# One more yield ahead of the packed values' products, in the attention that runs beside the mix products

## The chip, the cores and the metric

The kernel runs on one core of one Trainium2 chip. The metric is the device time of one execution in microseconds; the time of a kernel is the median of its runs. Five engines take part: TensorE (PE, with its weight loads as PEld), VectorE (DVE), ScalarE (ACT), GpSimd (POOL) and SyncE (SP), whose queue here only issues transfers.

## The reference

Three layers follow one another, for 8 batches of 576 tokens. The change lies in the first; what matters of it:

```python
def sm_attn(qq, kk, vv):
    s = scale * np.matmul(qq, kk.transpose(0, 1, 3, 2))
    s = s - np.max(s, axis=-1, keepdims=True)
    a = np.exp(s)
    a = a / (np.sum(a, axis=-1, keepdims=True) + 1e-09)
    return np.matmul(a, vv)
p_packed = sm_attn(p, k, v)        # 32 packed rows for each of 8 heads
out = sm_attn(q, p_packed, p_packed)
```

The second layer takes the real part of a Fourier transform over tokens and channels, adds it to its input, norms the sum, and sends it through two matrices with a rectifier between (512 to 2048 to 512). The third routes each token to one of eight experts and runs the expert's two matrices.

## The kernel before

Batch 0 is computed first, by its own function. From then on TensorE runs through a list of mixes: mix b is the second layer's pair of matrices for 512 tokens of batch b, and two half mixes (R0, R1) take the tokens that are left over of four batches each. A mix has 16 blocks `f`. `mm1` computes `hp` (L1193: 12 products of 128x128 by 128x512 out of `ut`, the normed and transposed tokens), ScalarE and VectorE rectify and split it into `ht` (L1200, L1201), and two blocks later `mm2` adds it into the four `acc` (L1213: 12 products). Values are held as two float16 parts, a high and a low one, so each product is done in three passes. After the last block VectorE adds the four `acc` to the tokens (L1221).

The attention and the Fourier part of batch b+1 are a Python generator, `attention(b + 1)`, that runs in the background of mix b. While the mix emits its products, `tick` is called after each third of a block; it advances the background generators to their next `yield`. The attention's rate is `ATT_RATE = 2.3` steps for 12 mix products. A `yield` so decides how many mix products stand between two steps of the attention in the order of the program. The framework then schedules each engine's instructions from this order, by priorities (`high_priority` lifts a few), and inserts the semaphores. When a mix begins, what is left of the last attention is emitted in one go (`drain`).

In the attention, heads are handled in two groups of four (`hf` 0 and 1). In order: the scores of the packed rows (`scores`, L385), their maximum and exponentials, a transpose of the exponentials by SP's queue (`et`, L408), and the packed values: `pps`, 30 products for each half (L440) of `et` and of `vhl`, the values split in two float16 parts by ScalarE (L428) and VectorE (L430). `split_q` splits the queries (ScalarE L363, GpSimd L364; only from batch 2 on), `load_q` loads them. Then come the second attention (`eh`, made by ScalarE and GpSimd at L561 and L563, and its products `bp` at L590), the Fourier part (`P` at L650 and L655, `X` at L660 and L705), its sum with the tokens (L711), and `norm`: statistics (L738, L739), `rstd` (L740, L742), the normed rows `un` (VectorE L746), their split (ScalarE L750, GpSimd L751) and the transpose into `ut` by SP's queue (L753). `ut` of batch b+1 is what mix b+1 reads.

During mix 0 the weights of the second layer are still being made: VectorE decodes them tile by tile (L311, L313, L315) and splits them (L281, `w`), together with ScalarE (L279). Later mixes read them ready, and other background work (the experts' weights, L337 to L342) runs instead. `after_mix` computes the routing logits (`lp`, L1241) and writes the tokens to `XS` (L1258, L1259, L1271).

Of the kernel before, what the change touches and what calls it, by code (L numbers as in the profile page):

```python
# [192 lines left out]
def _build(tc, nc, ctx, A, stop):  # L193
# [152 lines left out]
    def attention(b):  # L346
# [5 lines left out]
        def load_q(hf):  # L352
            qt = ap.tile([128, 2, 710], F32, tag="qkv", name=f"q{b}_{hf}", bufs=2)
            nc.sync.dma_start(qt, A["qd"][b, :, 2 * hf:2 * hf + 2])
            q32.append(qt)

        def split_q(hf):
            qt = q32[hf]
            if b < PLAIN:
                return  # L360
            pool, tag = (ap, "vhl") if hf else (wp, "UT")
            qh = pool.tile([128, 2, 2, 710], F16, tag=tag, name=f"qh{b}_{hf}", bufs=2 - hf)
            nc.scalar.copy(qh[:, 0], qt)  # L363
            nc.gpsimd.tensor_tensor(qh[:, 1], qt, qh[:, 0], op=ALU.subtract)  # L364
            qts.append(qh)
# [60 lines left out]
        for hf in range(2):  # L426
            vh = ap.tile([128, 2, 5, 256], F16, tag="vhl", name=f"vhl{b}_{hf}")
            nc.scalar.activation(vh[:, 0], vts[hf], AF.Copy, scale=256.0)  # L428
            yield
            nc.vector.scalar_tensor_tensor(vh[:, 1], vts[hf], 256.0, vh[:, 0], ALU.mult, ALU.subtract)  # L430
            load_q(hf)
            yield
            if hf == 1:
                split_q(0)
                yield
            n = 0
            for t in range(5):
                for (x, y) in PASS:
                    for h in range(2):
                        nc.tensor.matmul(pps[64 * h:64 * h + 64, 128 * hf:128 * hf + 128],  # L440
                                         ets[hf][:, 5 * x + t, 64 * h:64 * h + 64],
                                         vh[:, y, t, 128 * h:128 * h + 128], start=n == 0, stop=n == 14,
                                         skip_group_check=True)
                    n += 1
            yield
# [179 lines left out]
        for t in (2, 0, 1) if b % 4 == 3 else (0, 1, 2):  # L625
# [73 lines left out]
            for lu, ut in ((1, uu), (0, ul)):  # L699
                if t < 2:  # L700
                    for n in range(6):
                        hf, x, y = terms[n]
# [983 lines left out]
    for b in [0, 1, 2, "R0", 3, 4, 5, 6, "R1", 7]:  # L1686
# [16 lines left out]
        if not isinstance(b, str):  # L1703
            if b + 1 < NB:
                ga = attention(b + 1)
                bg.append([ga, 0.0, ATT_RATE])
            if b == 1:
                bg.append([ew, 0.0, EW_RATE])
            if b == 7:
                actx.close()  # L1710
                open_moe()
                drain(ew)
                drain(last)
                r0 = routing(0)
                bg.append([r0, 0.0, R0_RATE])
# [99 lines left out]
```

## Time and profile before

| | |
|---|---|
| median of 3 runs | 1394.88 us (1393.84 to 1395.7) |
| the profiled execution | 1394.49 us |
| its span | 1392.5 us |
| TensorE busy | 1358.9 us, 98% of the span |
| VectorE, ScalarE, GpSimd busy | 50%, 37%, 28% |
| mean granted TensorE clock | 0.995 |

The span is the time from the first to the last recorded instruction. A busy share is a mean over the whole program; which engine the others wait for differs from stage to stage, and the list of waits and the timeline of a stage tell it. In a timeline a row may stand for several instructions of a kind (x12), and the brackets at its end give the engine's idle time before it and what ended that.

### The profile page before, as it was taken

How to read it: one execution, taken by the hardware profiler on the slowest of the kernel's cores; microseconds unless marked ns; L12 is line 12 of the kernel's file. 1: busy time of each engine (PE TensorE's matmuls, PEld its weight loads, DVE VectorE, ACT ScalarE, POOL GpSimd, SP SyncE). 2: the span in 40 equal slices, each digit the busy share in tenths (PEclk: the TensorE clock that was granted, in tenths of full speed). 3: DMA queues.
4: the chain of work that ended last, by engine and by line, in shares of the span. 5: the costliest groups of instructions: out<-in, count | busy, mean ns of one | idle time of the engine just before them, and what ended most of it. 6: DMA issues, size and time to landing. Idle time of an engine off the chain costs nothing. (4 is left out here: it accounts for less than half of the span.)

```text
span 1392.5 us, 29837 instructions
## 1 busy us (share of the span) xinstructions
PE 1358.9 (98%) x11860; PEld 785.9 (56%) x11860; DVE 696.1 (50%) x1478; ACT 515.2 (37%) x949; POOL 389.4 (28%) x388
## 2 busy tenths in 40 slices
PE   7999999999999999999999999999999999999998
PEld 4554445445564544544544556445777777777675
DVE  6889857657534656665665654443841111111111
ACT  3533265455355545545545545211211111111111
POOL 2002244343422443444344343001122211212101
PEclk8999999999999999999999999999999999999999
DMA  7466395684567557658557456245959668958783
GB/s 267 173 221 188 92 253 141 159 233 124 134 177 212 160 140 218 158 148 223 145 151 206 131 144 167 62 184 150 289 126 331 153 192 247 262 144 234 240 268 128
DMA packets 219648, 256.75 MB, mean 184 GB/s; under 512 B 151663, under 2 KB 163055, under 8 KB 216816
## 3 DMA queue, kind: packets, MB, share of 16 engines
q1 hardware_dynamic: 213424, 235.39, 59.8%
q0 software_dynamic: 6080, 19.40, 4.3%
q8 instruction: 95, 1.56, 0.5%
q14 instruction: 49, 0.40, 0.1%
HBM read 267.52 MB, written 52.95 MB: 230 GB/s over the span
## 5 line engine op out<-in xcount | busy, mean ns | idle before, releaser
L1213 PE MATMUL acc<-w,ht 128*128 128x512 f16 x1728 | 414.2, 379 | 0.0
L1193 PE MATMUL hp<-ut,w 128*128 128x512 f16 (+1 forms) x1536 | 364.4, 378 | 4.3 <-DVE w L281 2.0
L1193 PEld LDWEIGHTS <-w 128*128 128x128 f16 x1920 | 181.2, 98 | 183.0 <-issue 9.3
L1213 PEld LDWEIGHTS <-ht 128*128 128x128 f16 x1728 | 164.0, 98 | 188.5 <-issue 10.2
L339 POOL TENSOR_TENSOR halfs<-stage,halfs 128x512 f16<-128x512 f32 x128 | 155.2, 1221 | 285.7 <-ACT halfs L338 269.0
L1631 PE MATMUL ehp<-xgt,w1b 128*128 128x128 f16 (+1 forms) x3936 | 218.5, 215 | 2.9 <-remote 1.7
L1631 PEld LDWEIGHTS <-w1b 128*128 128x128 f16 x3936 | 209.8, 98 | 18.1 <-issue 4.5
L1663 PE MATMUL eo<-w2b,hx 128*128 128x512 f16 (+1 forms) x984 | 209.5, 380 | 0.0
L1648 DVE SCALAR_TENSOR_TENSOR hx<-ehp,hx 128x512 f16<-128x512 f32 x76 | 52.4, 691 | 308.0 <-ACT hx L1647 283.7
L1201 DVE SCALAR_TENSOR_TENSOR ht<-hp,ht 128x512 f16<-128x512 f32 (+1 forms) x160 | 101.4, 634 | 163.3 <-ACT ht L1200 162.4
L1200 ACT ACTIVATE ht<-hp 128x512 f16<-128x512 f32 (+1 forms) x160 | 88.0, 550 | 243.8 <-PE hp L1193 238.7
L1663 PEld LDWEIGHTS <-hx 128*128 128x128 f16 (+1 forms) x984 | 87.2, 99 | 95.5 <-issue 4.4
L1673 POOL DMA_INDIRECT out<-ys,sidx x38 | 40.4, 1064 | 320.5 <-ACT ys L1672 300.3
L1647 ACT ACTIVATE hx<-ehp 128x512 f16<-128x512 f32 x76 | 45.3, 597 | 160.7 <-PE ehp L1631 154.1
L1672 ACT ACTIVATE ys<-eo,scl 128x512 f32<-128x512 f32 x38 | 26.1, 687 | 174.0 <-PE eo L1663 173.3
L338 ACT CAST halfs<-stage 128x512 f16<-128x512 f32 x128 | 77.1, 616 | 9.3 <-DMA WS<-halfs 5.9
L337 ACT ACTIVATE stage<-stage 128x512 f32<-128x512 f32 x128 | 77.5, 623 | 0.3
L1587 POOL DMA_INDIRECT xg<-XS,gidx x38 | 40.4, 1064 | 101.4 <-DVE sidx L1553 51.5
L364 POOL TENSOR_TENSOR qh<-q,qh 128x1420 f16<-128x1420 f32 x12 | 34.6, 2885 | 51.9 <-ACT qh L363 51.9
L1193 PE MATMUL hp<-utr,w 128*128 128x256 f16 x384 | 47.2, 273 | 0.5 <-DVE ht L1201 0.5
L555 POOL TENSOR_TENSOR eo<-ee 128x256 f32<-128x256 f32 (+1 forms) x21 | 21.0, 1001 | 59.9 <-DVE ee L539 59.3
L751 POOL TENSOR_TENSOR unh<-un,unh 128x512 f16<-128x512 f32 x28 | 31.9, 1159 | 18.3 <-ACT unh L750 14.6
(399 smaller groups left out, 1332.8 us busy)
## 6 DMA issues: line engine op xcount, KB each, us to landing
w1b<-WS SPq DMA_DIRECT2D x156, 512.0 KB
w2b<-WS SPq DMA_DIRECT2D x156, 512.0 KB
stage<-in_w SPq DMA_DIRECT2D x64, 512.0 KB
WS<-halfs SPq DMA_DIRECT2D x128, 256.0 KB
q<-in_qd SPq DMA_DIRECT2D x16, 710.0 KB
v<-in_vd SPq DMA_DIRECT2D x16, 640.0 KB
k<-in_kd SPq DMA_DIRECT2D x16, 576.0 KB
XS<-xh SPq DMA_DIRECT2D x36, 256.0 KB
```

The costliest lines, as they stand in the source:

```text
L337: nc.scalar.activation(st[:, a], st[:, a], AF.Copy, scale=64.0 if k < 4 else 256.0)
L338: nc.scalar.copy(so[:, 0], st[:, a])
L339: nc.gpsimd.tensor_tensor(so[:, 1], st[:, a], so[:, 0], op=ALU.subtract)
L1193: nc.tensor.matmul(hp[:, c0:ntok], w12[:, f, 0, x, 128 * c:128 * c + 128], ut[:, 4 * y + c, c0:ntok], start=n == 0, stop=n == 11, skip_gro ...
L1200: pace[1] = nc.scalar.activation(ht[:, 0, :ntok], hp[:, :ntok], AF.Relu).ins
L1201: pace[0] = nc.vector.scalar_tensor_tensor(ht[:, 1, :ntok], hp[:, :ntok], 0.0, ht[:, 0, :ntok], ALU.max, ALU.subtract).ins
L1213: nc.tensor.matmul(self.acc[j], ht[:, x, 128 * j:128 * j + 128], w12[:, f, 1, y], start=f == 0 and n == 0, stop=f == 15 and n == 2)
L1587: nc.gpsimd.indirect_dma_start(out=g_, out_offset=None, in_=XS[0:rows], in_offset=bass.IndirectOffsetOnAxis(ap=gidx[:, b:b + 1], axis=0), ...
L1631: latest[0] = nc.tensor.matmul(hp[:, cols], w1b[r][:, 2 * c + fg, x, 128 * f:128 * f + 128], xt[b][:, 4 * y + c, rows], start=c + n == 0 a ...
L1647: nc.scalar.activation(ht[:, fg, 0], hp, AF.Relu)
L1648: nc.vector.scalar_tensor_tensor(ht[:, fg, 1], hp, 0.0, ht[:, fg, 0], ALU.max, ALU.subtract)
L1663: latest[0] = nc.tensor.matmul(op[rows], h[:, f // 4, x, c0 + rows.start:c0 + rows.stop], w2b[r + a][:, f, y], start=n == 0, stop=n == 23, ...
```

## The change

It adds a `yield` in front of the packed values' products: for the second heads in every batch of the generator (1 to 7), and for the first heads in batches 4 to 7. Two lines are added, so that every later line has a number greater by two.

```diff
             if hf == 1:
                 split_q(0)
                 yield
+            if hf == 1 or b >= 4:
+                yield
             n = 0
             for t in range(5):
                 for (x, y) in PASS:
```

How the order of the instructions changes is seen at three places. The first is TensorE in batch 5, between the first heads' packed values (`vhl_0`) and the second heads' (`vhl_1`); `hp_4`, `hp_5` and `acc_5902` to `acc_5905` are the mix's tiles, `lp` the routing logits. Weight loads and repeats are left out. Before:

```order
L440 MATMUL pps_5993<-vhl_0_5994,et_0_5938 64x128
...
L1193 MATMUL hp_4_6043<-ut_5522,w_130 128x512
...
L1213 MATMUL acc_5902<-w_130,ht_2_5890 128x512
...
L1213 MATMUL acc_5904<-w_130,ht_2_5890 128x512
L440 LDWEIGHTS et_1_5971
L440 MATMUL pps_5993<-vhl_1_6054,et_1_5971 64x128
```

After:

```order
L442 MATMUL pps_5993<-vhl_0_5994,et_0_5938 64x128
...
L1195 MATMUL hp_4_6013<-ut_5533,w_130 128x512
...
L1215 MATMUL acc_5902<-w_130,ht_2_5890 128x512
...
L1215 MATMUL acc_5905<-w_130,ht_2_5890 128x512
...
L1245 MATMUL lp_6090<-wgh,xt_5964 128x9
...
L1195 MATMUL hp_5_6102<-ut_5533,w_130 128x512
L442 LDWEIGHTS et_1_5971
L442 MATMUL pps_5993<-vhl_1_6063,et_1_5971 64x128
```

Between the two halves stood 12 `hp` and 9 `acc` products; now 6 `hp`, 12 `acc` and 9 `hp` products do, with the routing logits among them.

The second place is VectorE at the end of batch 1's attention, which runs beside mix 0: the statistics, `rstd` and the two `un` of the batch's last two tiles, and the adds of mix 0's four accumulators (`acc_670` to `acc_673`). Before:

```order
L738 BN_STATS bst_1_0_1455<-ul_1_1348 128x6
L738 BN_STATS bst_1_1_1458<-uu_1_1349 128x6
L739 BN_AGGR mv_1_1453<-bst_1_0_1455 128x2
L739 BN_AGGR mv_1_1453<-bst_1_1_1458 128x2
L740 TENSOR_SCALAR rstd_1_1454<-mv_1_1453 128x2
L746 TENSOR_SCALAR un_1_0_1475<-ul_1_1348,mv_1_1453,rstd_1_1454 128x512
L746 TENSOR_SCALAR un_1_1_1487<-uu_1_1349,mv_1_1453,rstd_1_1454 128x512
...
L1221 TENSOR_TENSOR ul_0_457<-ul_0_457,acc_670 128x512
```

After:

```order
L740 BN_STATS bst_1_1_1467<-uu_1_1356 128x6
L741 BN_AGGR mv_1_1462<-bst_1_0_1464 128x2
L1223 TENSOR_TENSOR ul_0_457<-ul_0_457,acc_670 128x512
L741 BN_AGGR mv_1_1462<-bst_1_1_1467 128x2
L1223 TENSOR_TENSOR uu_0_458<-uu_0_458,acc_671 128x512
L742 TENSOR_SCALAR rstd_1_1463<-mv_1_1462 128x2
L1223 TENSOR_TENSOR ul_1_459<-ul_1_459,acc_672 128x512
L748 TENSOR_SCALAR un_1_0_1481<-ul_1_1355,mv_1_1462,rstd_1_1463 128x512
L748 TENSOR_SCALAR un_1_1_1494<-uu_1_1356,mv_1_1462,rstd_1_1463 128x512
L1223 TENSOR_TENSOR uu_1_460<-uu_1_460,acc_673 128x512
```

Three of the four adds now stand ahead of the two `un`; before, all four stood behind them.

The third place is TensorE over the same stretch, from the batch's last X product to the first product of mix 1 (`hp_0`); `ht_13` to `ht_15` are the last blocks of mix 0, `s_2_0_0` the scores of batch 2. Before:

```order
L705 MATMUL X_1_1_1411<-pph,big_957 128x128
L1213 LDWEIGHTS ht_13_1465
L1213 MATMUL acc_673<-w_130,ht_13_1465 128x512
...
L660 MATMUL X_2_1512<-pph,big_957 32x256
...
L385 MATMUL s_2_0_0_1658<-k_0_1654,p_1651 32x288 x4
L1213 LDWEIGHTS ht_15_1569
L1213 MATMUL acc_671<-w_130,ht_15_1569 128x512
...
L1193 MATMUL hp_0_1584<-ut_1322,w_130 128x512
```

After:

```order
L707 MATMUL X_1_1_1418<-pph,big_969 128x128
L1215 LDWEIGHTS ht_14_1505
L1215 MATMUL acc_673<-w_130,ht_14_1505 128x512
...
L662 MATMUL X_2_1515<-pph,big_969 32x256
...
L1215 MATMUL acc_671<-w_130,ht_15_1568 128x512
...
L385 MATMUL s_2_0_0_1658<-k_0_1654,p_1651 32x288 x4
L1195 LDWEIGHTS w_130
L1195 MATMUL hp_0_1584<-ut_1331,w_130 128x512
L385 MATMUL s_2_0_1_1659<-k_0_1654,p_1651 32x288 x4
```

The last X product has moved towards the end of the mix: 27 mix products stood between it and `hp_0` before, 13 do now, and one of the score groups stands behind the first product of `hp_0`.

## Rows read from the trace of the kernel before

**Rows 1.** The profile page: span, and busy time of each engine
```profile
span 1392.5 us, 29837 instructions
...
PE 1358.9 (98%) x11860; PEld 785.9 (56%) x11860; DVE 696.1 (50%) x1478; ACT 515.2 (37%) x949; POOL 389.4 (28%) x388
```

**Rows 2.** TensorE's waits: line, releaser, total us, times, longest us
```profile
PE hp L1193 <- DVE w L281: 2.0, 2, 1.8
...
PE pps L440 <- DVE vhl L430: 1.7, 2, 1.3
PE bp L590 <- POOL eh L563: 1.7, 2, 0.9
...
PE pps L440 <- DMA et<-ehl: 1.3, 1, 1.3
```

**Rows 3.** Timeline, batches 2 and 4: start, us, engine, work, [idle before, releaser]
```profile
195.77 0.97 PE L440 MATMUL pps<-vhl,et 128*64 128x128 f16 x28 [0.45 <-DVE vhl L430]
...
440.75 1.03 PE L440 MATMUL pps<-vhl,et 128*64 128x128 f16 x30 [1.33 <-DMA et<-ehl]
...
443.12 1.49 DVE L430 SCALAR_TENSOR_TENSOR vhl<-v,vhl 128x1280 f16<-128x1280 f32 x1 [3.01 <-ACT vhl L428]
443.13 1.37 ACT L363 CAST qh<-q 128x1420 f16<-128x1420 f32 x1
...
446.35 1.03 PE L440 MATMUL pps<-vhl,et 128*64 128x128 f16 x30
```

**Rows 4.** Timeline, batch 5, second heads
```profile
544.92 0.72 ACT L1258 ACTIVATE xh<-uu,rsc 128x512 f16<-128x512 f32 x1 [2.15 <-DMA XS<-xh]
...
548.55 1.49 DVE L430 SCALAR_TENSOR_TENSOR vhl<-v,vhl 128x1280 f16<-128x1280 f32 x1 [1.53 <-ACT vhl L428]
...
550.10 0.97 PE L440 MATMUL pps<-vhl,et 128*64 128x128 f16 x28 [1.28 <-DVE vhl L430]
```

**Rows 5.** Timeline, mix 0: twelve mix products in a row
```profile
109.43 2.75 PE L1213 MATMUL acc<-w,ht 128*128 128x512 f16 x12
```

**Rows 6.** Timeline, the turn from mix 0 to mix 1
```profile
161.57 8.38 SPq L753 DMA_TRANSPOSE ut<-unh  x4
...
164.13 3.41 PE L1213 MATMUL acc<-w,ht 128*128 128x512 f16 x15
164.81 0.55 DVE L746 TENSOR_SCALAR un<-ul,mv,rstd 128x512 f32<-128x512 f32 x1 [0.81 <-POOL rstd L742]
...
166.15 2.27 POOL L751 TENSOR_TENSOR unh<-un,unh 128x512 f16<-128x512 f32 x2 [1.22 <-ACT unh L750]
...
167.36 0.69 DVE L1221 TENSOR_TENSOR ul<-ul,acc 128x512 f32<-128x512 f32 x1
...
167.47 0.69 PE L385 MATMUL s<-k,p 64*32 64x288 f32 x8
...
168.09 1.90 PE L1213 MATMUL acc<-w,ht 128*128 128x512 f16 x8
...
171.91 1.89 PE L1193 MATMUL hp<-ut,w 128*128 128x512 f16 x8 [1.92 <-DMA ut<-unh]
```

**Rows 7.** Windows, mix 0: stretch, length, busy PE PEld DVE ACT POOL, clock, DMA share, GB/s
```profile
106.00:118.00 12.00, 12.00 (x58) 5.13 (x54) 12.00 (x18) 4.99 (x7) 1.55 (x1) 1.00 0.50 181
...
142.00:154.00 12.00, 11.79 (x78) 6.56 (x75) 11.57 (x20) 6.08 (x12) 1.79 (x1) 1.00 0.50 171
```

**Rows 8.** The same windows at the program's start and at the turn of mix 0
```profile
25.00:30.00 5.00, 3.49 (x7) 2.52 (x8) 4.76 (x11) 1.10 (x2) 1.23 (x2) 0.50 0.38 127
30.00:35.00 5.00, 5.00 (x23) 2.85 (x22) 4.79 (x10) 1.18 (x2) 0.85 (x4) 0.74 0.00 0
...
170.00:175.00 5.00, 3.09 (x19) 1.17 (x20) 3.64 (x9) 0.00 (x0) 0.00 (x0) 1.00 0.28 53
```

**Rows 9.** Timeline, a later turn (SP's queue and TensorE)
```profile
720.93 3.49 SPq L753 DMA_TRANSPOSE ut<-unh  x2
...
730.32 2.75 PE L1193 MATMUL hp<-ut,w 128*128 128x512 f16 x12
```

## The prediction

> **What bounds the kernel now.** The page comes first: TensorE is busy for 1358.9 us of a span of 1392.5 us, every other engine for half of it or less [rows 1]. The rest, 33.6 us, is all that any order of the same work can win, so the question is only which TensorE waits the change takes away and which it makes. The list of waits by engine and line names them [rows 2]. At the line of the packed values (`pps`) TensorE waits three times: twice for `vhl`, the split of the values, 1.7 us together, and once for `et`, the transposed exponentials, 1.3 us. Exactly: 0.45 us in batch 2, 1.33 us before the first heads of batch 4 [rows 3] and 1.28 us before the second heads of batch 5 [rows 4]; 3.06 us in all. All other entries of that list are waits of the mix, of the Fourier part or of the turn from one mix to the next.
>
> A step of the attention generator is handed out per 12/2.3, about 5 to 6, mix products, and 12 such products take 2.75 us with the last one's own time, some 0.22 us each [rows 5]. One extra yield is therefore some 1.3 us of TensorE work that has no need of the attention.
>
> **The change, part by part.** It adds or removes no instruction. TensorE's busy time stays at 1358.9 us; the sum is made of waits alone.
>
> Second heads, all batches. In batch 5, 21 mix products stand between the two halves of `pps` in the order of before and 27 after, six more, 1.3 us. The wait there is 1.28 us, because ScalarE stood 2.15 us for a buffer that a transfer to XS had to free, and so the split on VectorE ran only from 548.55 us to 550.04 us [rows 4]. ScalarE and VectorE do not wait for the first half of `pps` here, so the split ends at the same time and the six products lie in front of it: −1.28 us. Batch 2 likewise, −0.45 us. Batches 3, 6 and 7 have no wait there to lose.
>
> First heads, batches 4 to 7. In batch 4 the first heads' products wait 1.33 us for `et` [rows 3]; six products of 1.3 us go ahead of them: −1.33 us, and nothing in batches 5 to 7, where TensorE did not wait. There is a price in batch 4: ScalarE now has the split of q (`qh`, 1.37 us at 443.13 us) ahead of the split of the second heads' values, which costs VectorE's split the same 1.37 us of delay; it had landed at 444.61 us against products at 446.35 us, a margin of 1.74 us, and six products more. I take nothing for it, and 1.0 us as the other end.
>
> Later steps. All that follows in the attention moves back by 6 products (batches 2 and 3) or 12 (4 to 7): the loads of q, p, k and v on SP's queue, the splits on ScalarE and GpSimd, the second attention and the Fourier part. The transfers are for a batch that TensorE reads tens of us later. What stands at the end is the turn: the next mix's first product needs `ut`, the transposed norm. At the tightest turn of batches 2 to 7, SP's last transposes end at 724.42 us and the mix starts at 730.32 us [rows 9]; with the 1.96 us from the end of issue to landing that the turn of mix 0 shows (below) there are 3.9 us left, and the Fourier part moves by 9 products, 2 us. I take nothing; the three other turns of this kind have more room, and two are followed by a half mix, whose products need another `ut`.
>
> Batch 1, whose attention runs beside mix 0, is where I see a loss. It too gets the yield before the second heads, but it has no room. VectorE decodes the weights there and is busy for 12.00 of 12 us and still 11.57 of 12 later [rows 7], and TensorE's waits of mix 0 come of it: 2.0 us for weight tiles, 1.8 us of them at one place, and 1.7 us for `eh`, which ScalarE and GpSimd make of what VectorE hands on [rows 2]; 3.7 us in all. The change moves each of these places. In the order of after, VectorE does the split of that one weight tile before it waits for the next stage, so that I take its 1.8 us as gone; the others, 1.9 us, I leave, since their cover is the same in steps and VectorE is as full. Bounds: 1.0 us left (half of the others goes too) to 3.7 us (nothing goes).
>
> The turn of mix 0 then costs more. Before, TensorE waited 1.92 us for `ut` [rows 6]. The chain: VectorE writes the normed rows `un` at 164.81 us, ScalarE and GpSimd split them until 168.42 us, SP transposes them until 169.95 us, and the product starts at 171.91 us: 7.1 us from the start of `un`. TensorE had 15 + 8 products and 8 score products (0.69 us) [rows 6] besides the P and X products to fill it. After, 13 mix products instead of 27 stand behind the last X of the batch; and in VectorE's order the two `un` now stand behind three of mix 0's closing adds (0.69 us each, as the one at 167.36 us), the third of which needs the products of `ht_15` up to the third column block. So `un` can't start before TensorE has only 3 products (0.66 us) and four score products (0.35 us) left. From there: one add 0.69 + 0.2 to see it, 7.1 us of chain, against 1.0 us of cover: a wait of 7.0 us in place of 1.92 us, +5.1 us. With mix 0's other waits at 1.9 us in place of 3.7 us (−1.8 us) that is +3.3 us; with the bounds above +2.4 to +5.1 us, and +1.9 us if the add is not in the way.
>
> A small wait may appear at one of the many moved places; I take one of the size of the shorter `vhl` wait, +0.4 us, 0 to 1.0 us.
>
> Sum: −3.06 + 3.3 + 0.4 = +0.6 us on the profiled execution's 1394.49 us: 1395.1 us. The median of the runs is 0.39 us above that execution, so 1395.5 us. The low ends (+1.9 and 0) give −1.2 us, 1393.7 us; the high ones (+5.1, 1.0, and 1.0 for batch 4) +4.0 us, 1398.9 us.
>
> **A rule to weigh.** What would a wait of 7 us do to TensorE's clock? The granted clock was 1.00 (2.4 GHz) in the stretch with the wait of 1.92 us [rows 8]; near the start, where TensorE was busy for only 3.49 us of 5, it was 0.50 (1.2 GHz), and it came back within the following 5 us of full work (0.74 on the mean, so 2.6 us at half). A loss of that sort after the turn would cost half of 2.6, 1.3 us. The Trainium skill ("TensorE: Matmul & The Clock Gate", section "The HAM clock gate (the "warmup" mystery)") says that an idle TensorE falls to half clock and that activity has to release it again. By that rule the change is dearer by those 1.3 us; by the row of the 1.92 us wait it isn't. The forecast leaves the loss out, because the score products split the wait.
>
> **The rivals.** (A) *Faster.* The moved places in mix 0 lose nearly all their waits, as batch 1's steps no longer meet VectorE's late tiles, and the turn grows less, to 5.5 us, as the transposes meet an emptier queue: −3.7 + 3.6 − 3.06 = −3.2 us, 1391.7 us with the median's 0.39 us. For it: the largest wait of mix 0 goes by the order itself. Against: VectorE is full from 106 to 154 us [rows 7], and the chain from `un` has no slack that a queue could give. It decides once mix 0 with its turn costs less than +0.3 us net.
>
> (B) *Slower by the clock.* The turn's wait of 7 us drops the clock, 1.3 us, and mix 0 keeps its other waits: +5.1 + 1.3 + 0.4 − 3.06 = +3.7 us, 1398.6 us. At most, if half clock holds for the 5 + 2.6 us that it does in [rows 8], 3.8 us instead of 1.3 us: 1401.1 us. It decides once the wait at the turn is seen with a granted clock below 1.
>
> (C) *Slower by the tiles.* VectorE's full stretch of mix 0 gets the norm and the adds later, and new waits for weight tiles appear, two of the size of the 1.8 us: +3.3 + 3.5 + 0.4 − 3.06 = +4.1 us, 1399.0 us. For: VectorE is saturated from 106 to 154 us; against: in before one tile alone came late by more than 0.3 us.
>
> (D) *The change doesn't do what it says.* The splits move along with the products (ScalarE does `vhl` of the second heads only when it sees the first half of `pps` end, as in batch 4, where its copy of them starts behind the first half), and half of the 3.06 us remains: +1.5 us on the forecast, 1397.0 us.
>
> **How the numbers follow.** Forecast 0.52, A 0.14, B 0.13, C 0.10, D 0.11. What a measurement can tell from no change is about 0.2%, 2.8 us: faster is below 1392.1 us, slower above 1397.7 us. Of the forecast's 0.52, 0.05 ends above and 0.01 below; of A's 0.14, 0.11 is faster; of B and C together, 0.20 is slower; of D, 0.02. Faster 0.12, slower 0.27, the rest, 0.61, the same. The range leaves out A's far end and the dear end of B and C: 1391.9 to 1399.2 us. The forecast alone: 1393.7 to 1398.9 us.
>
> **What would show it.** Right: no wait of over 0.3 us at the `pps` line of batches 2, 4 and 5; a wait for `ut` of about 7 us at the end of mix 0, with VectorE's `un` behind the third closing add; the wait of 1.8 us for a weight tile gone; from the second mix on, the same sequence of waits as before less those three. Wrong: a turn below 5 us (then A); a granted clock below 1.00 in the 5 us behind the turn (B); more than 3.7 us of waits in mix 0 ahead of the turn (C); a split of `vhl` that starts later beside its products (D). The forecast fails above all if the turn's chain is shorter than the one I copy from before.

## The result: 0.56% slower, outside the range

The changed kernel takes 1400.68 us (median of 5 runs, 1399.69 to 1401.8) against 1393.9 us for the kernel before in runs taken with it (1391.84 to 1395.7): a ratio of 1.0056 with a 95% interval of 1.0043 to 1.0068. Forecast were 1395.5 us and a range up to 1399.2 us. The profiled execution took 1400.68 us.

The page of the changed kernel, its span and TensorE's busy time, against [rows 1]:

```profile
span 1398.9 us, 29822 instructions
...
PE 1361.6 (97%) x11860; PEld 784.7 (56%) x11860; DVE 696.5 (50%) x1478; ACT 515.7 (37%) x949; POOL 387.1 (28%) x388
```

The span is 6.4 us longer. TensorE's busy time, which the change does not touch in instructions, is 2.7 us longer; its idle time went from 33.6 to 37.3 us, 3.7 us. So over a third of the loss isn't waiting at all: the same products took longer.

TensorE's waits in the changed kernel (line, releaser, total, times, longest), against [rows 2]:

```profile
PE s L385 <- issue: 3.5, 1, 3.5
PE bp L592 <- POOL eh L565: 3.2, 2, 2.5
PE hp L1195 <- DMA ut<-unh: 2.8, 1, 2.8
PE hp L1195 <- ACT w L279: 2.4, 3, 1.5
...
PE pps L442 <- DVE vhl L430: 0.9, 1, 0.9
```

The packed values (`pps`) wait 0.9 us instead of 3.06 us: in this execution the change did what it says there, all but one wait. Mix 0's waits for `eh` (L592) and for weight tiles (`hp` on L279) are 5.6 us instead of 3.7 us (3.9 us with a wait of 0.2 us for L279 that the prediction leaves out). The turn of mix 0 stands in two rows, 3.5 us at the scores (L385) and 2.8 us for `ut`. Its timeline, against [rows 6]:

```profile
170.30 2.12 PE L1215 MATMUL acc<-w,ht 128*128 128x512 f16 x9
...
171.16 0.69 DVE L1223 TENSOR_TENSOR uu<-uu,acc 128x512 f32<-128x512 f32 x1 [0.55 <-PE acc L1215]
...
171.84 0.68 DVE L1223 TENSOR_TENSOR ul<-ul,acc 128x512 f32<-128x512 f32 x1
...
172.74 0.55 DVE L748 TENSOR_SCALAR un<-ul,mv,rstd 128x512 f32<-128x512 f32 x1 [0.23 <-POOL rstd L744]
...
174.08 2.27 POOL L753 TENSOR_TENSOR unh<-un,unh 128x512 f16<-128x512 f32 x2 [1.22 <-ACT unh L752]
...
175.37 0.41 DVE L694 TENSOR_TENSOR ru<-P,qs 32x256 f32<-32x256 f32 x1
...
175.87 1.18 PE L385 MATMUL s<-k,p 64*32 64x288 f32 x8 [3.46 <-issue]
...
179.90 0.58 PE L1195 MATMUL hp<-ut,w 128*128 128x512 f16 x1 [2.84 <-DMA ut<-unh]
```

Three of mix 0's closing adds now run ahead of the normed rows `un`, the second at 171.16 us and the third at 171.84 us. By the row of `un`, its last wait is for GpSimd's `rstd`, which ended at 172.71 us; the VectorE step that feeds it (L742, 171.77 us) stands behind the second add, which had waited 0.55 us for `acc`. The third add was done at 172.52 us, 0.2 us too early to matter. TensorE, idle from 172.42 us, starts the next mix at 179.90 us: 7.16 us from the start of `un`, as before (7.1 us). For the wait ahead of the scores the profile names no releaser; they start within 0.1 us of the end of L694 (175.78 us), the last reader of a `P` tile, and in the program the score tiles take turns with `P` and `X` in the same two buffers.

The clock at the turn (stretch, its length, busy time of PE, PEld, DVE, ACT, POOL, granted clock, DMA share, GB/s), against [rows 8]; first one window of the kernel before, behind its own turn, then the changed kernel:

```profile
175.00:180.00 5.00, 5.00 (x35) 2.05 (x34) 3.65 (x13) 4.57 (x10) 0.00 (x0) 1.00 0.53 171
```

```profile
170.00:175.00 5.00, 2.42 (x17) 0.89 (x11) 4.21 (x10) 1.14 (x2) 1.71 (x3) 1.00 0.33 62
175.00:180.00 5.00, 1.29 (x9) 0.33 (x9) 4.22 (x11) 0.69 (x1) 1.50 (x3) 0.53 0.57 105
180.00:185.00 5.00, 5.00 (x18) 1.40 (x17) 2.74 (x7) 2.50 (x7) 0.00 (x0) 0.50 0.39 132
185.00:190.00 5.00, 5.00 (x34) 1.98 (x33) 3.62 (x9) 2.37 (x5) 0.00 (x0) 0.94 0.79 200
```

It falls to half (1.2 GHz of 2.4 GHz) within the wait and stays there until behind 185 us, while TensorE is busy for 5.00 of 5 us. This is not one odd execution: the mean granted clock over a whole run is 0.989 to 0.992 in the five runs of the changed kernel, and 0.992 to 0.998 in the 62 runs of the kernel before that stand beside the experiments below.

A second place, 127 us into the program, shows the other wait of mix 0. First GpSimd's low part of `eh` at this place in the kernel before, then the changed kernel's rows and its clock:

```profile
121.19 1.36 POOL L563 TENSOR_TENSOR eh<-eo,eh 128x512 f16<-128x512 f32 x1 [5.30 <-ACT eh L561]
```

```profile
123.68 1.21 DVE L281 SCALAR_TENSOR_TENSOR w<-raw,w 128x1024 f16<-128x1024 f32 x1
...
123.97 3.10 POOL L565 TENSOR_TENSOR eh<-eo,eh 128x512 f16<-128x512 f32 x1 [5.76 <-ACT eh L563]
124.82 1.21 DVE L313 SCALAR_TENSOR_TENSOR halfs<-stage,halfs 128x1024 int32<-128x1024 int32 x1
125.95 1.14 DVE L539 TENSOR_SCALAR m<-m 128x16 f32<-128x16 f32 x1
...
127.12 0.42 PE L592 MATMUL bp<-cst,eh 128*128 128x289 f16 x2 [2.50 <-POOL eh L565]
...
127.63 3.97 PE L1195 MATMUL hp<-ut,w 128*128 128x512 f16 x10
```

```profile
127.00:129.00 2.00, 1.88 (x7) 0.85 (x8) 2.00 (x6) 0.00 (x0) 0.06 (x1) 0.63 0.99 418
129.00:131.00 2.00, 2.00 (x6) 0.67 (x5) 1.19 (x3) 0.00 (x0) 0.73 (x1) 0.51 0.05 16
```

GpSimd's low part of `eh` (L565) took 3.10 us beside VectorE's L281 and L313, against 1.36 us before; the products waited 2.50 us for it, the clock fell to half just behind that wait, and the ten mix products took 3.97 us, against 2.32 us before.

The stretches of the program show where the time goes. Mix 1 starts 8.0 us later than before (179.90 against 171.91 us), mix 2 10.3 us later (283.01 against 272.66 us). TensorE is busy for 1.8 us more up to mix 1 and for 2.9 us more during it, the two stretches in which the clock fell, and for 1.9 us less in all that follows. So the 2.7 us are a balance: from these two stretches, the slow clock's part is an estimated 4.7 us.

### The profile page after: what moved, and what is told of

Read it like the earlier page. It is cut to its first block, busy times and chain, and to the rows that moved or that the text cites. A ratio compares the mean times of both kernels' runs of the same rounds, so it can differ in the third digit from the quotient of the medians.

```text
span 1398.9 us, 29822 instructions
## 1 busy us (share of the span) xinstructions
PE 1361.6 (97%) x11860; PEld 784.7 (56%) x11860; DVE 696.5 (50%) x1478; ACT 515.7 (37%) x949; POOL 387.1 (28%) x388
## 5 line engine op out<-in xcount | busy, mean ns | idle before, releaser
L1195 PE MATMUL hp<-ut,w 128*128 128x512 f16 (+1 forms) x1536 | 369.4, 381 | 5.3 <-DMA ut<-unh 2.8
L1195 PEld LDWEIGHTS <-w 128*128 128x128 f16 x1920 | 180.4, 98 | 189.3 <-issue 20.7
L1195 PE MATMUL hp<-utr,w 128*128 128x256 f16 x384 | 47.5, 273 | 0.6 <-DVE ht L1203 0.6
```

What stands on the lines that cost most here:

```text
L1195: nc.tensor.matmul(hp[:, c0:ntok], w12[:, f, 0, x, 128 * c:128 * c + 128], ut[:, 4 * y + c, c0:ntok], start=n == 0, stop=n == 11, skip_gro ...
```

## The experiments

Every time stands beside runs of the kernel before on the same chip. Its median there was 1393.64, 1391.22 and 1393.92 us in the three groups that follow, so kernels of different groups are compared by their ratios. (From the first product of the second half mix to TensorE's last one, work that no version touches, the profiles took 505 to 512 us; so the totals of two profiles aren't compared.)

**Without batch 1.** The yield of batch 1 is left out.

```diff
-            if hf == 1 or b >= 4:
+            if (hf == 1 and b >= 2) or b >= 4:
```

> The change without its yield in batch 1. Theory (the whole loss is batch 1's: its later steps make TensorE wait in mix 0 and at the turn, and the waits drop the clock): mix 0 and its turn are as before (waits of 3.7 us and 1.9 us there, granted clock 1.00), the packed values' waits fall from 3.06 us to the 0.9 us that the changed kernel still has in batch 4, so about 2.2 us faster than before, 1391.7 us. Rival (the later batches' shifts bear a part of the loss): above 1394 us, with waits at later turns that the kernel before has not.

Measured: 1393.41 us, ratio 0.9999 (0.9988 to 1.0011). The loss is gone with batch 1's yield, and the later batches show none of their own; but the gain of 2.2 us is not there either. Two things in the profile speak to that. The first product of mix 1 waits as before, but this time the clock falls behind the wait (0.71 on the mean in the window):

```profile
171.16 2.72 PE L1195 MATMUL hp<-ut,w 128*128 128x512 f16 x8 [1.96 <-DMA ut<-unh]
```

```profile
170.00:175.00 5.00, 3.84 (x17) 1.09 (x18) 2.34 (x4) 0.00 (x0) 0.00 (x0) 0.71 0.10 20
```

And batch 5's second heads wait again. ScalarE's wait for the transfer to XS, ahead of their split, was 2.15 us in [rows 4], 1.03 us in the changed kernel's profile and is 2.33 us here. The changed kernel, then this one:

```profile
557.19 0.72 ACT L1260 ACTIVATE xh<-uu,rsc 128x512 f16<-128x512 f32 x1 [1.03 <-DMA XS<-xh]
```

```profile
548.49 0.72 ACT L1260 ACTIVATE xh<-uu,rsc 128x512 f16<-128x512 f32 x1 [2.33 <-DMA XS<-xh]
...
552.47 0.97 PE L442 MATMUL pps<-vhl,et 128*64 128x128 f16 x28 [0.71 <-DVE vhl L430]
```

The profiles of the other versions follow this: with both batch 1's yield and the later ones, ScalarE's wait for XS is 1.0 to 1.2 us and batch 5 has no wait (six profiles); with the later ones alone it is 2.3 to 2.6 us and 0.71 to 1.53 us of batch 5's wait stay (three). Why batch 1's yield shortens that transfer's wait was not traced.

**Batch 1 alone.**

```diff
-            if hf == 1 or b >= 4:
+            if hf == 1 and b == 1:
```

> Only batch 1's yield. Theory: all of the changed kernel's loss and none of its gain: two waits of 2.5 and 1.5 us in mix 0, 6.3 us at the turn in two pieces, half clock behind both; 9 us slower than before, 1403 us. Rival (batch 1 bears only what the waits show, without the clock): 6 us slower, 1400 us. Rival (the later batches bear it): below 1397 us.

Measured: 1403.2 us, ratio 1.0064 (1.0051 to 1.0077), 9 us. The theory's time; its largest wait is the one at the scores, and those for `eh` and `ut` are the changed kernel's to a tenth:

```profile
PE s L385 <- issue: 4.1, 3, 3.5
```

Batch 1's one yield alone gives the whole loss; its interval and the whole change's overlap.

**A part of the turn filled.** 24 more products that nobody reads, 23 of them in the gap.

```diff
         for f in range(LEAD):
...
+        if b == 1:
+            junk = psO.tile([128, 512], F32, tag="o", name="junk")
+            for k in range(24):
+                nc.tensor.matmul(junk, w12[:, 0, 0, 0, :128], UT[0][:, 0], start=k == 0, stop=k == 23)
```

> The change, with 24 further products of 128x512 (23 of them in the order between mix 0's last product and mix 1's first, into a tile that nobody reads; results unchanged). They need 5.2 us of TensorE, which the 6.3 us of waits have room for. Theory (an idle TensorE loses its clock at the turn, and that costs about 3.1 us behind it): granted clock 1.00 from 172 to 186 us, the first mix product at the same 179.9 us, and 3.1 us faster than the changed kernel, 1397.6 us; the loss at 127 us stays. Rival (the slow products behind the turn have another cause, or the added products lengthen the turn by as much): 1400.7 us or more.

Measured: 1399.71 us, ratio 1.0037 (1.0025 to 1.005). This does not decide it: 2.44 us of the turn's wait were still unfilled, and the clock fell within a microsecond behind that rest.

```profile
178.23 0.38 PE L1195 MATMUL hp<-ut,w 128*128 128x512 f16 x1 [2.44 <-DMA ut<-unh]
```

```profile
125.00:130.00 5.00, 3.58 (x18) 1.76 (x19) 4.48 (x8) 0.69 (x2) 1.80 (x2) 1.00 0.64 219
...
175.00:180.00 5.00, 2.56 (x15) 0.72 (x14) 2.55 (x10) 0.74 (x2) 0.00 (x0) 0.90 0.67 67
180.00:185.00 5.00, 5.00 (x29) 1.82 (x28) 3.83 (x9) 2.85 (x7) 0.00 (x0) 0.76 0.86 236
```

It shows something else: in this execution the same 2.50 us wait for `eh` left the clock at 1.00 (the window from 125 us), and the ten products behind it took 2.32 us instead of 3.97 us:

```profile
126.42 0.42 PE L592 MATMUL bp<-cst,eh 128*128 128x289 f16 x2 [2.50 <-POOL eh L565]
...
126.89 2.32 PE L1195 MATMUL hp<-ut,w 128*128 128x512 f16 x10
```

**The normed rows first.** Mix 0's closing adds are held behind batch 1's last `un` on VectorE.

```diff
+            if nm == '1_1' and j:
+                last_un.append(ins.ins)
...
+                    with tc.issue_after(last_un.pop()) if last_un else nullcontext():
```

> The change, with mix 0's closing adds held behind batch 1's last two normed rows in VectorE's order; TensorE's order is the same. Theory (three adds, the third waiting for TensorE, hold the normed rows back): the normed rows start at 171.0 us in place of 172.7 us, mix 1 starts 1.7 us earlier, and the time is 1399.0 us or, if the clock no longer drops, 1396 us. Rival (the transposes or GpSimd set the turn, whatever VectorE's order): mix 1 starts at 179.9 us as in the changed kernel, 1400.7 us.

Measured: 1400.04 us, ratio 1.0042 (1.0029 to 1.0054), by the ratios 2 us below the changed kernel, with overlapping intervals. The times so don't decide it; the trace shows the order's effect:

```profile
169.64 2.12 PE L1218 MATMUL acc<-w,ht 128*128 128x512 f16 x9
...
170.44 0.55 DVE L749 TENSOR_SCALAR un<-ul,mv,rstd 128x512 f32<-128x512 f32 x1 [0.81 <-POOL rstd L745]
...
177.62 1.01 PE L1198 MATMUL hp<-ut,w 128*128 128x512 f16 x2 [1.07 <-DMA ut<-unh]
```

`un` starts at 170.44 us instead of 172.74 us, mix 1 at 177.62 us instead of 179.90 us, 7.2 us behind it again. (TensorE ended mix 0 at 171.76 us instead of 172.42 us here, so that 1.6 us of it are due to the order.) The clock fell all the same.

**The turn filled.** The gap is filled with 30 products into the accumulator of mix 1's first product, which fixes their place.

```diff
+            if f == 0 and UT.get(1) is ut:
+                for k in range(30):
+                    nc.tensor.matmul(hp, w12[:, 0, 0, 0, :128], UT[0][:, 0], start=k == 0, stop=k == 29)
```

(For this, mix 0's last two blocks are emitted ahead of mix 1's first ones. No run has this without the added products. But the changed kernel's trace already has mix 0's last nine products, at 170.30 us, ahead of mix 1's first, so it should move little there.)

> The change, with the turn of mix 0 filled: 30 further products of 128x512 (6.5 us) into the accumulator of mix 1's first product, which then overwrites it; results unchanged, and their place ahead of the first product is fixed. Theory (idle time takes the clock): granted clock 1.00 from 170 to 190 us, the first mix product no more than 0.5 us later than in the changed kernel, the products behind it at full speed, and 3 us faster than the changed kernel, 1397.5 us. Rival (the clock behind the turn does not hang on TensorE's idle time): clock of 0.5 as in the changed kernel, 1400.7 us.

Measured: 1397.26 us, ratio 1.004 (1.0028 to 1.0053): 2.2 us below the changed kernel by the ratios, of 3 us expected, with intervals that overlap.

```profile
172.10 0.55 DVE L748 TENSOR_SCALAR un<-ul,mv,rstd 128x512 f32<-128x512 f32 x1 [0.23 <-POOL rstd L744]
...
179.81 1.03 PE L1198 MATMUL hp<-ut,w 128*128 128x512 f16 x4
```

```profile
175.00:180.00 5.00, 4.88 (x33) 1.77 (x32) 4.81 (x13) 1.33 (x2) 0.86 (x2) 1.00 0.56 105
180.00:185.00 5.00, 4.86 (x34) 1.89 (x33) 3.74 (x12) 2.79 (x7) 0.00 (x0) 1.00 1.10 245
```

The added products end and the real ones begin at 179.81 us, 7.7 us behind `un`: half a microsecond later than without them. The granted clock is 1.00 in all windows of the turn. So the clock there hangs on TensorE's idle time. Its price is seen best from mix 1's first product to mix 2's: 103.1 us in the changed kernel, 101.5 us here, although a new wait of 1.17 us for `ht` stands in this stretch. By the run times alone this version, the partly filled one and the one with the normed rows first (ratios 1.0040, 1.0037 and 1.0042) can't be told apart.

**`eh` by VectorE.** In batch 1, VectorE makes the low parts instead of GpSimd.

```diff
-                nc.gpsimd.tensor_tensor(eh[:, 512:], eo, eh[:, :512], op=ALU.subtract)
+                (nc.vector if b == 1 else nc.gpsimd).tensor_tensor(eh[:, 512:], eo, eh[:, :512], op=ALU.subtract)
```

> The change, with the low parts of the second attention's values (eh) in batch 1 made by VectorE in place of GpSimd; TensorE's order of batch 1 then has the last X product at product 380 of mix 0, as in the kernel before (381), and VectorE's normed rows stand ahead of all closing adds. Theory (GpSimd's part, 3.1 us long beside VectorE's work, makes the wait of 2.5 us, and the late order the wait at the turn): the wait for eh falls to 1 us or less, the turn to some 2 us, both without a lost clock: 8 us below the changed kernel, 1392.5 us. Rival (VectorE is full, and one more operation of 0.7 us on it makes waits for weight tiles instead): 1397 us or more.

Measured: 1389.75 us, ratio 0.999 (0.998 to 1.0): some 9 us below the changed kernel by the ratios, and all of batch 1's yield is still in it.

```profile
PE hp L1195 <- DMA ut<-unh: 1.8, 1, 1.8
```

```profile
132.84 1.71 PE L592 MATMUL bp<-cst,eh 128*128 128x289 f16 x6 [3.48 <-ACT eh L563]
...
134.56 4.00 PE L1195 MATMUL hp<-ut,w 128*128 128x512 f16 x9
```

The wait for GpSimd is gone and the turn is back at 1.8 us, with a clock of 1.00. A wait of 3.5 us for ScalarE's second part of `eh` stands in their place, and behind it, against the expectation, the clock fell: nine products took 4.00 us. This run changes GpSimd's part and the order of the rest together, so it does not tell one from the other. It does show that batch 1's yield can stand without the long turn. Mix 0, from its first product at L1195 to mix 1's, is 118.3 us long here, against 122.4 us in the changed kernel and 114.2 us before; where the rest of the 9 us lies was not traced.

**Without batch 1, the turn filled.** The first experiment, with 8 products as above in the 2 us that are left of the turn.

> The change without batch 1's yield, and the 2 us wait at the turn of mix 0 filled with 8 further products (1.7 us); results unchanged. Its companion without them measured no gain, and its profile has a granted clock of 0.71 behind a wait of 2.0 us at the turn. Theory (that clock loss of about 1.5 us eats the gain at the packed values in many of the executions): 1.5 us below it and 1.7 us below the kernel before, 1391.9 us, with less spread. Rival (the gain at the packed values is not there): 1393.5 us.

Measured: 1388.88 us, ratio 0.9984 (0.997 to 0.9998), 1387.01 to 1392.56 us. This interval and the first experiment's (0.9988 to 1.0011) overlap. In the two profiles mix 1, from its first product to mix 2's, took 102.5 us there and 100.7 us here. The window in which the first experiment's clock was 0.71:

```profile
170.00:175.00 5.00, 4.74 (x30) 1.70 (x32) 4.17 (x14) 1.52 (x4) 0.00 (x0) 1.00 0.36 87
```

**Batch 4's split of q later.** ScalarE's copy of q in batch 4 is held behind that of the second heads' values (one run).

```diff
             if hf == 1:
-                split_q(0)
+                if b != 4:
+                    split_q(0)
                 yield
...
+        if b == 4:
+            with tc.issue_after(vl.ins):
+                split_q(0)
```

> The change, with batch 4's first split of q held behind the split of the second heads' values on ScalarE, as it was before. Theory (GpSimd's split of q runs beside VectorE's split of the values and makes it 3.1 us long in place of 1.5 us): VectorE's split takes 1.5 us and the wait of 0.9 us at the second heads of batch 4 is gone. Rival (ScalarE's later copy alone makes the wait): VectorE's split still takes 3.1 us or the wait stays.

Measured: 1396.15 us in the one run. The place in the changed kernel, then in this one:

```profile
454.26 2.89 POOL L364 TENSOR_TENSOR qh<-q,qh 128x1420 f16<-128x1420 f32 x1 [3.11 <-ACT qh L363]
...
455.38 3.11 DVE L430 SCALAR_TENSOR_TENSOR vhl<-v,vhl 128x1280 f16<-128x1280 f32 x1 [5.72 <-ACT vhl L428]
...
458.55 0.97 PE L442 MATMUL pps<-vhl,et 128*64 128x128 f16 x28 [0.91 <-DVE vhl L430]
```

```profile
450.85 1.49 DVE L430 SCALAR_TENSOR_TENSOR vhl<-v,vhl 128x1280 f16<-128x1280 f32 x1 [2.88 <-ACT vhl L428]
...
452.78 2.89 POOL L364 TENSOR_TENSOR qh<-q,qh 128x1420 f16<-128x1420 f32 x1 [3.33 <-ACT qh L363]
...
455.57 1.03 PE L443 MATMUL pps<-vhl,et 128*64 128x128 f16 x30
```

VectorE's split, 3.11 us beside GpSimd's, is 1.49 us once GpSimd starts behind it, and the wait is gone. The edit takes away ScalarE's delay of the split as well; but a split of 1.49 us from 455.38 us on would have ended at 456.87 us, and TensorE only began to wait at 457.64 us, so the lengthening is what makes the wait.

**The kernel before, the turn filled** (8 products as above).

> The kernel before, with the 1.9 us wait at the turn of mix 0 filled with 8 further products (1.7 us); results unchanged. Theory (the same wait sometimes costs the clock, 1.5 us, and the later yields are worth about 2 us by themselves): between 0 and 1.5 us below the kernel before, and so 1 to 2 us above the kernel that has the later yields and the filled turn. Rival (the filled turn is all of that kernel's gain, the later yields give nothing): 2.2 us below the kernel before.

Measured: 1392.2 us, ratio 0.999 (0.9976 to 1.0003). A gain of 1.4 us by the ratio, not clear of none, and less than that with the later yields, though the two intervals overlap.

**All three together:** no yield in batch 1, the turn filled with 8 products, batch 4's split later.

> The change without batch 1's yield, with the turn of mix 0 filled with 8 products and batch 4's first split of q held behind the split of the second heads' values; results unchanged. Theory (each of the three waits goes by its own cause): no wait at the packed values of batch 4, ratio to the kernel before 0.998, some 3 us below it. Rival (the gains do not add): 0.999 or above.

Measured: 1390.52 us, ratio 0.9968 (0.9957 to 0.998), 3.4 us below the kernel before by the medians and 4.5 us by the ratio. Of all versions this one is furthest below the kernel before; the filled version without batch 1 is just below it as well (its interval ends at 0.9998).

```profile
PE pps L443 <- DVE vhl L430: 1.3, 1, 1.3
```

Mix 0 waits as in [rows 2] (2.0 us for L281, 1.7 us for `eh`), the turn no longer, and of the packed values only batch 5's wait is left, as long as before in spite of the six products more.

## Why the prediction was wrong

**The packed values: right in kind, 0.9 us too good.** Of 3.06 us, 2.15 us went, in this pair of executions. The other profiles show less: the waits at the packed values are 3.06, 2.36 and 1.83 us in the three without the later yields, 0.62 to 2.35 us in the nine with them, 1.2 us less on the mean. What stayed is batch 4's second heads, for which the prediction took "nothing" with 1.0 us as the other end. It saw the copy on ScalarE come first, but not that GpSimd's split of q then runs from 454.26 to 457.15 us beside VectorE's split, which so took 3.11 us instead of 1.49 us; the experiment on batch 4 shows it. The Trainium skill ("SBUF — State Buffer", section "Who interferes with whom") says that VectorE and GpSimd share a pair of ports as an exclusive lock, and that a VectorE instruction with two inputs in SBUF contends with a GpSimd instruction that reads SBUF. The trace agrees: from GpSimd's end at 457.15 us to VectorE's at 458.49 us are 1.34 us, about one undisturbed split. And in batch 5 the cover hangs on ScalarE's wait for XS: "the split ends at the same time and the six products lie in front of it" left no wait in the versions that keep batch 1's yield, where ScalarE's wait was 1 us shorter too, and 0.71 to 1.53 us in the three without it. For the changed kernel that term so came out partly by luck.

**The turn of mix 0: right in kind and nearly in size.** 7.0 us were forecast, 6.3 us of waits measured, +4.4 us for +5.1 us; the chain from `un` was 7.16 us against 7.1 us. Holding the adds back moved `un` and the next mix together. Two steps were read wrongly. The four score products of the order are eight in the trace, 0.69 us and not 0.35 us, and covered 1.18 us at half clock. And `un` waited for the second add, by way of `rstd`, not for the third; the two paths ended within 0.2 us of each other, so that the start of `un` came out right by luck. The low end of +1.9 us was not worked out: without the add's 0.9 us the same sum gives +2.4 us.

**Mix 0 ahead of the turn: the step that failed first.** "The others, 1.9 us, I leave, since their cover is the same in steps and VectorE is as full", and the tile's 1.8 us "as gone". Measured were 3.2 us for `eh` and 2.4 us for tiles, 5.6 us against a bound of 3.7 us: a term of −1.8 us became +1.9 us. The one tile's wait did go, as forecast, but another of 1.5 us, on ScalarE's part of a tile (L279, at 89.24 us), came in its place. The wait for `eh` grew from 0.9 to 2.5 us at its longest, with GpSimd's part beside two of VectorE's operations in a row. That the one engine lengthens the other's operation is shown for batch 4; here the trace suits it, and no run changed that alone. More than 3.7 us of waits ahead of the turn was the sign of rival (C), given 0.10; of its two new waits for tiles one came, and the wait for `eh` grew in place of the other.

**The clock: the step that failed worst.** "The forecast leaves the loss out, because the score products split the wait." They did split it, and it fell: 0.53, 0.50 and 0.94 in three windows behind 175 us, and once more behind the wait for `eh`. TensorE's busy time grew by 2.7 us, for a term of 0: by 4.7 us up to the end of mix 1, less 1.9 us behind it. Filling the turn kept 1.00; by the ratios it gave back 2.2 us, with intervals that overlap, and by the trace 1.6 us of mix 1. That is rival (B), given 0.13, by its mechanism. Its place and its sign were named, its second place was not, and its price of 1.3 us was too small; its dear end, 1401.1 us, lies close to the 1400.68 us measured. The row on which the forecast leaned as well, a clock of 1.00 behind a wait of 1.92 us, was one execution: the first experiment shows 0.71 behind 1.96 us at the same place. The Trainium skill's rule ("TensorE: Matmul & The Clock Gate", section "The HAM clock gate (the "warmup" mystery)"), that idleness throttles and activity has to release, agrees with these rows, and was the better guide than the row.

The sum as it came, from the profiles: −2.15 + 4.4 + 1.9 + 2.7 = +6.9 us, against 6.4 us of the span. The rest, −0.5 us, is in other waits and was not traced to a cause; neither were the 1.9 us by which TensorE's busy time fell behind mix 1, some 1.1 us of them in the last stretch, which the change does not touch.

**The later batches: right that they cost nothing, too good on their gain.** Without batch 1 nothing is lost, and no later turn shows a wait for `ut`. How much the later yields gain by themselves stays open within 2 us: the ratio is 0.9999 with them, and 0.9984 with the turn filled against 0.999 for the filled turn alone.

## What to carry to other kernels

A shift by a few products in the order is worth what the waits at its own place say, but its price is set elsewhere: look at each chain that ends in a fixed hand-over (here the last normed rows ahead of the next mix) and at the stage whose other engine is full. Let the forecast of a TensorE wait like those here (2 to 6 us) hold a term for the products behind it at half clock, and take one execution's clock for no proof. Where idle time can't be removed, filling it with products that nobody reads kept the clock here in all four versions that did it; by the ratios the three that have a counterpart without it were 1.4 to 2.2 us faster, a gain that none of these pairs shows clear of noise by itself.

## What the runs showed of the hardware

The length of a wait did not decide whether the clock fell: 1.92 us left it at 1.00 and 1.96 us gave a window of 0.71; the same 2.50 us gave ten products in 3.97 us in the changed kernel and in 2.32 us in another. Of the six profiles with that wait, five show half clock behind it. And beside each other VectorE and GpSimd took longer by about a whole instruction: VectorE's split 3.11 us instead of 1.49 us, GpSimd's `eh` 3.10 us instead of 1.36 us, and VectorE's small L539 beside that `eh` 1.14 us, where its median in this run is 0.17 us.
